# An mLSTM cell and a GELU feed-forward block on one core: the down projection as seven block products, and a new order for the first chunk

## The chip, the cores and the metric

The kernel runs on one core of one Trainium2 chip. The metric is the device time of an execution in microseconds. The core has TensorE (matmuls, with a separate row "PEld" for loading the stationary operand), VectorE (DVE), ScalarE (ACT), GpSimd (POOL) and SyncE (SP), which here only issues DMAs. Before the change, three runs took 579.77 us in the median (578.19 to 583.44).

## What is computed

The reference, cut to what matters:

```python
# q, k, v, o_gate: (4, 8, 768, 40); i_gate, f_gate: (4, 8, 768); B=4, H=8, S=768, D=40
for t in range(S):
    m_new = np.maximum(f_gate[:, :, t] + m, i_gate[:, :, t])
    f_stab = np.exp(f_gate[:, :, t] + m - m_new)
    i_stab = np.exp(i_gate[:, :, t] - m_new)
    C = f_stab * C + i_stab * outer(v_t, k_t)
    n = f_stab * n + i_stab * k_t
    y[:, :, t] = sigmoid(o_gate_t) * (C @ q_t) / np.maximum(np.abs(n . q_t), 1.0)
x = y.transpose(0, 2, 1, 3).reshape(3072, 320)
h = x @ w_in                                   # w_in: (320, 2048), float64
g = 0.5 * h * (1.0 + erf(h / np.sqrt(2.0)))
out = (g @ w_out).astype(np.float32)           # w_out: (2048, 320), float64
```

## The kernel before

**Chunks.** The sequence of 768 steps is cut into six chunks of 128. Within a chunk the recurrence is done as matrix products: scores between all pairs of steps, weighted by exponentials of the gates and masked to the past, plus the contribution of a state that is carried from chunk to chunk. So each chunk c has three parts: the cell (batch by batch, b = 0 to 3), the up projection of its 4 x 128 = 512 tokens with the GELU, and the down projection. The cell of chunk c+1 is computed while chunk c is projected down (for chunk 0, already while it is projected up).

**The order is written by hand.** A string of letters sets the program order of every engine (`play`, L463); there is no automatic scheduling, and every engine works through its own instructions in that order. FIRST holds the cell of chunk 0, UP_0 and DOWN_0 the projections of chunk 0 with the cell of chunk 1, DOWN (used for chunks 1 to 4) the down projection of a chunk with the cell of the next; the up projections of chunks 1 to 5 are eight U in a row, and the last chunk's down projection stands alone. For the cell of batch b: M masks on GpSimd (L289), W computes the weights as eight Exps on ScalarE (L310; in chunk 0 from a matmul that spreads rows of M, L307), T transposes keys and queries on TensorE (L323) with copies by ScalarE (L326), G is the output gate's sigmoid on ScalarE (L316), S the scores (L336) and their weighting on VectorE (L339), C the carry: state times queries (L359), new state (L354), and the state's decay on GpSimd (L372) and addition on VectorE (L373); V the values (L381, L384), Y the finishing chain (L391 on GpSimd, L393 to L398 on VectorE) and X the transposes of y into `xT` (L409, copied by VectorE L410 and ScalarE L411), after which the next inputs are loaded (L122, SyncE's queue). D turns the gates' factors (L192, L202). P, K and L are the fetching of weight pieces (L230), their conversion from float64 bits to float32 (L241 to L255, VectorE and ScalarE) and the input loads; R stores M to DRAM and B loads rows of it, spread over the partitions (L133).

**Up (U, L417 to L428).** One step computes two column blocks of 128 hidden units for 512 tokens: five blocks of 64 rows, alternating between the two halves of the array, into two PSUM banks of 512 columns; ScalarE writes the Gelu of both into `g`, whose layout is (128 hidden units, 16 blocks f, 512 tokens).

**Down (F, L432 to L461).** In chunk 0 a step is one block f for four batches, since the weights arrive block by block (L440). From chunk 1 on a step is four blocks of one batch (L455): 16 matmuls of 128x128 by 128x320 add up in one bank, ScalarE copies it out (L447) and SyncE stores it. That is 16 steps, 64 matmuls a chunk.

**PSUM.** There are eight banks: two for transposes (`ps_tr`), two for carries and values (`ps_h`), and four (`ps_mm`, tag "mm") which scores, up steps and down steps take in turn.

Of the kernel before, what the change touches and what calls it, by code (L numbers as in the profile page):

```python
# [21 lines left out]

FIRST = """
    W0 T0 P W1 W2 D L1 P K M0 P P T1 S0 V0 M1 L2 R C0 K S1 G0 V1 M2 K G1 T2 Y0 K G2 X0 W3 L3 K S2 L4 C1 B4 V2 Y1 X1
    T3 G3 M3 Y2 B5 S3 L5 C2 B7 V3 K C3 Y3 B6 X2 X3"""
UP_0 = """
    M0 T0 K G0 U L6 W0 S0 M1 C0 W1 M2 T1 M3 U K K U S1 V0 W2 L8 C1 U K W3 T2 K U K L7 Y0 K U U K K U T3 G1 V1 L9 S2
    G2 S3 K C2 V2 K Y1 F F Y2 X0 F K F F K K X1 F K C3"""
DOWN_0 = """
    V3 K F K F X2 F F F F G3 K K K F F Y3 K F X3 F"""  # L30
DOWN = """
    M0 T0 W0 F F M1 M2 T1 W1 W2 F S0 C0 F M3 T2 W3 G0 G1 G2 G3 F S1 C1 V0 Y0 F F T3 F S2 C2 V1 Y1 F
    X0 F S3 C3 V2 Y2 F X1 F V3 Y3 F X2 F F X3 F"""
# [3 lines left out]
def kernel(  # L37
# [31 lines left out]
    NLD = 6  # L69
    NM = 4  # L70
    NB = 4
    WP = 512
    assert S % L == 0 and DFF % (4 * WP) == 0 and DM % R == 0 and DM <= WP and D <= DP and NLD > B == NM == 4
# [9 lines left out]
    ps_mm = ctx.enter_context(tc.tile_pool(name="ps_mm", bufs=4, space=bass.MemoryType.PSUM))  # L83
# [27 lines left out]
    M_d = dram.tile([NCH - 1, BH, L], F32, name="M_d")  # L111
# [15 lines left out]
    def load_M(n):  # L127

        if n >= NCH * B:
            return  # L130
        c, b = divmod(n, B)
        Mb[n] = wts.tile([P, H, L], F32, name="Mb", tag="Mb", bufs=NM)
        nc.sync.dma_start(out=Mb[n].rearrange("p h l -> p (h l)"),  # L133
                      in_=M_d[c - 1, b * H:(b + 1) * H, :].rearrange("h l -> (h l)").unsqueeze(0).to_broadcast([P, H * L]))
# [34 lines left out]
    for c0, c1 in ((0, 1), (1, NCH)):  # L169
# [5 lines left out]
        for c in range(c0, c1):  # L175
            nc.vector.tensor_tensor_scan(out=M[:, c], data0=a[:, c], data1=a[:, c], initial=m0[:, c:c + 1],
                                         op0=OP.max, op1=OP.max)
            if c + 1 < NCH:
                nc.vector.tensor_tensor(out=m0[:, c + 1:c + 2], in0=bl[:, c, L - 1:L], in1=M[:, c, L - 1:L],
                                        op=OP.add)  # L180
    nc.vector.tensor_tensor(out=ew, in0=a[:, 0:NCH - 1],
# [32 lines left out]
    for f0 in range(0, DFF, 2 * WP):  # L214
        for blk in range(NK):
            src = w_src["in"][blk * R:(blk + 1) * R, 2 * f0:2 * (f0 + 2 * WP)]
            pieces.append(([src[:, 2 * WP * e:2 * WP * (e + 1)] for e in range(2)], w_in[:, blk, f0 // 2:f0 // 2 + WP]))
# [52 lines left out]
    def store_M():  # L270
        nc.sync.dma_start(out=M_d.rearrange("c p l -> p c l"), in_=M[:, 1:NCH])
# [7 lines left out]
    class Cell:  # L279
# [6 lines left out]
        def mask(self, b):  # L286

            t, fill = (Mb[self.c * B + b], 1.0e30) if self.c > 0 else (W[b], 0.0)
# [3 lines left out]
        def weights(self, b):  # L292
# [3 lines left out]
            if self.c > 0:  # L296
                M_n = Mb.pop(n)
            for h in range(H):
                r = b * H + h
                if self.c > 0:  # L300
# [215 lines left out]
```

## Time and profile before

| what | value |
|---|---|
| median of three runs | 579.77 us |
| the profiled execution | 579.88 us |
| its span, first to last instruction | 578.2 us |
| granted clock of TensorE (mean) | 0.999 |
| up projections start (chunks 0 to 5) | 61.92, 152.43, 241.17, 329.90, 418.64, 505.51 us |
| last chunk's down projection starts | 540.04 us |

A row of the timeline gives start, duration, engine, line, operation, what is written from what, shapes and count, and in brackets what ended the idle time before it. A float32 matmul appears as two rows of MATMUL (and two of LDWEIGHTS), since it is done in two passes; a transpose appears as one. Durations of matmuls include the time in the array and overlap, so distances between starts say more than durations. The windows view gives the busy time of each engine in a stretch.

### The profile page before, as it was taken

What the parts mean: (1) busy time and instruction counts of PE and PEld (TensorE: products, weight loads), DVE (VectorE), ACT (ScalarE), POOL (GpSimd) and SP (SyncE); (2) the same over time, 40 slices, a digit from 0 to 9 for tenths busy, and PEclk for the clock granted to TensorE, in tenths of its full rate; (3) what the DMA queues carried; (4) which work ended last, traced back from release to release, by engine and by line L of the source; (5) the groups of instructions that cost most, each with busy time, mean ns of one, the idle gap of its engine ahead of it and who ended that gap; (6) DMA issues with size and microseconds to landing.
All of it is one profiled execution on the core that took longest, in us unless ns stands there. A gap on an engine that the chain in (4) does not pass through costs nothing.

```text
span 578.2 us, 9535 instructions
## 1 busy us (share of the span) xinstructions
PE 558.8 (97%) x3914; PEld 365.5 (63%) x3914; DVE 200.8 (35%) x444; ACT 238.8 (41%) x524; POOL 82.1 (14%) x130
## 2 busy tenths in 40 slices
PE   5888899999999999999999999999999999999997
PEld 4877654776544777644778644677744677744675
DVE  6387586699300146300137300136400035300000
ACT  3567899544422841232850223750232761232100
POOL 3212320123000122300112300032300001000000
PEclk9999999999999999999999999999999999999999
DMA  9839979669300325700225800126100000000000
GB/s 158 144 84 189 238 175 207 136 133 194 70 1 0 118 62 83 115 1 1 86 73 93 126 0 1 56 103 92 24 11 1 0 14 12 12 12 1 0 23 24
DMA packets 110396, 41.54 MB, mean 72 GB/s; under 512 B 101168, under 2 KB 104400, under 8 KB 110352
## 3 DMA queue, kind: packets, MB, share of 16 engines
q1 hardware_dynamic: 110352, 40.92, 35.7%
q8 instruction: 31, 0.51, 0.4%
q14 instruction: 13, 0.11, 0.1%
HBM read 36.90 MB, written 4.01 MB: 71 GB/s over the span
## 4 chain that ended last, share of the span: by engine, by line
PE 90%; DVE 6%; ACT 2%; issue 1%; DMA 0%; SPq 0%; DVEq 0%; ACTq 0%
PE pu L425 35%; PE po L455 31%; PE ps L336 5%; PE ph L381 4%; PE pt L323 4%; PE po L440 3%; PE pm L307 2%; PE px L409 2%; PE pf L359 2%; PE pf L354 2%; DVE sig L248 1%; DVE pow L253 1%; DVE W L339 1%; DVE w_out L255 1%; DVE sig L246 0%
## 5 line engine op out<-in xcount | busy, mean ns | idle before, releaser
L425 PE MATMUL pu<-xT,w_in 64*128 64x512 f32 x960 | 209.9, 591 | 0.5 <-ACT g L428 0.4
L455 PE MATMUL po<-w_out,g 128*128 128x320 f32 x640 | 183.2, 436 | 0.0
L425 PEld LDWEIGHTS pu<-xT,w_in 64*128 64x128 f32 x960 | 94.5, 187 | 111.2 <-issue 106.9
L455 PEld LDWEIGHTS po<-w_out,g 128*128 128x128 f32 x640 | 117.4, 190 | 44.2 <-issue 0.8
L339 DVE TENSOR_TENSOR W<-ps,W 128x512 f32<-128x512 f32 x48 | 30.8, 685 | 245.4 <-PE ps L336 239.7
L428 ACT ACTIVATE g<-pu 128x512 f32<-128x512 f32 x96 | 52.1, 594 | 126.9 <-PE pu L425 126.8
L411 ACT COPY xT<-px 64x384 f32<-64x384 f32 (+1 forms) x48 | 17.9, 420 | 101.4 <-DVE xT L410 101.4
L372 POOL TENSOR_TENSOR state<-state,dec 64x164 f32<-64x164 f32 x32 | 15.1, 470 | 254.1 <-PE pf L359 252.9
L310 ACT ACTIVATE W<-Mb,aT 128x128 f32<-128x128 f32 x160 | 48.4, 392 | 0.1
L391 POOL TENSOR_TENSOR ob<-hs,ob 128x320 f32<-128x320 f32 x24 | 19.9, 829 | 135.9 <-ACT ob L316 70.5
L440 PE MATMUL po<-w_out,g 128*128 128x320 f32 x128 | 35.9, 435 | 0.8 <-DVE w_out L255 0.8
L381 PE MATMUL ph<-vb,W 128*64 128x41 f32 x768 | 29.7, 239 | 2.6 <-DVE W L339 1.5
L336 PEld LDWEIGHTS ps<-qT,kT 64*128 64x128 f32 x384 | 26.3, 204 | 9.3 <-issue 6.6
L447 ACT COPY o_sb<-po 128x320 f32<-128x320 f32 x24 | 10.1, 425 | 53.1 <-PE po L455 38.2
L336 PE MATMUL ps<-qT,kT 64*128 64x128 f32 x384 | 30.8, 302 | 0.7 <-ACT qT L326 0.7
L381 PEld LDWEIGHTS ph<-vb,W 128*64 128x64 f32 x768 | 27.2, 148 | 5.9 <-DVE W L339 2.7
L440 PEld LDWEIGHTS po<-w_out,g 128*128 128x128 f32 x128 | 23.8, 190 | 10.5 <-DVE w_out L255 1.3
L410 DVE COPY xT<-px 64x384 f32<-64x384 f32 (+1 forms) x48 | 20.9, 475 | 14.7 <-PE px L409 14.3
L243 ACT ACTIVATE pow<-pow,e_hi 128x320 f32<-128x320 uint32 (+1 forms) x26 | 16.2, 623 | 17.4 <-DVE pow L241 17.4
L289 POOL TENSOR_SCALAR_AFFINE_SELECT Mb<-Mb 128x1024 f32<-128x1024 f32 x20 | 22.7, 1160 | 2.9 <-DMA Mb<-M_d 2.7
L409 PE MATMUL px<-ident,ob 128*128 128x128 f32 x120 | 18.6, 287 | 4.1 <-DVE ob L397 3.8
L326 ACT COPY kT<-pt 128x512 f32<-128x512 f32 x24 | 14.0, 582 | 17.5 <-PE pt L323 17.4
(78 smaller groups left out, 433.1 us busy)
## 6 DMA issues: line engine op xcount, KB each, us to landing
Mb<-M_d SPq DMA_DIRECT2D x20, 512.0 KB, 3.9
bits<-in_moe_w_in_dram SPq DMA_DIRECT2D x20, 256.0 KB, 5.1
bits<-in_moe_w_out_dram SPq DMA_DIRECT2D x16, 320.0 KB, 3.4
qb<-in_q_dram SPq DMA_DIRECT2D x24, 160.0 KB, 4.3
kb<-in_k_dram SPq DMA_DIRECT2D x24, 160.0 KB, 4.7
vb<-in_v_dram SPq DMA_DIRECT2D x24, 160.0 KB, 5.2
ob<-in_o_gate_dram SPq DMA_DIRECT2D x24, 160.0 KB, 3.7
out_dram<-o_sb SPq DMA_DIRECT2D x24, 160.0 KB, 1.8
```

The lines of the kernel that those rows point to most:

```text
L289: nc.gpsimd.affine_select(out=t, in_=t, compare_op=OP.is_ge, fill=fill, base=0, pattern=[[0, H], [1, L]], channel_multiplier=-1)
L310: nc.scalar.activation(out=W[n][:, h, :], in_=src, func=AF.Exp, scale=-1.0, bias=aT[:, self.c, r:r + 1])
L323: nc.tensor.transpose(pt[:, p, :], src[n % NLD][:, 2 * p:2 * p + 2, :].rearrange("p h d -> p (h d)"), ident)
L336: nc.tensor.matmul(ps[hip][:, p, :], kT[r, p, :], qT[r, p, :], start=True, stop=True)
L339: nc.vector.tensor_tensor(out=w, in0=ps[hip], in1=w, op=OP.mult)
L381: nc.tensor.matmul(ph[r, h, :], Pm[:, h, r], vb[n % NLD][:, h, :], start=True, stop=True)
L409: nc.tensor.transpose(px[:, k, :], ob[n % NLD][:, (k0 + k) * R:(k0 + k + 2) * R], ident)
L410: nc.vector.tensor_copy(out=xT[0:R, k0:k0 + m, t], in_=px[0:R])
L425: nc.tensor.matmul(pu[e], w_in[r, blk, i * P:(i + 1) * P], xT[r, (blk - e) % NK, :], start=(blk == 0), stop=(blk == NK - 1))
L428: nc.scalar.activation(out=g[:, f + e * (WP // P), :], in_=pu[e], func=AF.Gelu)
L440: nc.tensor.matmul(hold["po"][b], g[:, f, b * L:(b + 1) * L], w_out[:, f, :], start=(f == 0), stop=(f == NF - 1))
L455: nc.tensor.matmul(po, g[:, f, b * L:(b + 1) * L], w_out[:, f, :], start=(f == 0), stop=(f == NF - 1))
```

## The change

The down projection of chunks 1 to 5 is done as a product of matrices in two-by-two blocks with seven block products in place of eight. The block rows are the two halves of the 512 tokens (h), the inner blocks the two halves of the 16 hidden blocks (e, eight each), the block columns the two halves of the 320 outputs (n). One block product is, for each of two token groups t, eight matmuls of 128x128 by 128x160, so 7 x 2 x 8 = 112 matmuls; a step F is one product for one t, and there are 14.

- After each up step VectorE forms three sums of 128x256: s1 = a21 + a22, then a11 - a21 in place of a21, then s2 = s1 - a11. They live in the four buffers that held raw weight bits. A fourth, a12 - s2 (two instructions of 128x1024), is formed in place after the second product that is read out by ScalarE (`p2`).
- After chunk 0, `weight_sums` forms the four combinations of w_out's blocks: 32 sums of 128x160 on VectorE.
- The products use two banks under tag "b", two products after one another adding into one bank: P1 then P2, P6 alone, P5 then P3, P7 then P4. What is read out in between: `p1` and `p2` are copies on ScalarE, `p6`, `p5`, `p7`, `p3` and `p4` are additions on VectorE. Outputs are stored for two batches at once, after P3 and after P4.
- PSUM: the four banks of tag "mm" become two of tag "a" (scores, even up steps, half of chunk 0's output) and two of tag "b" (odd up steps, products, the spread rows of M, the transposes X of chunk 0).
- Block f of `g` and the pieces of w_in are renumbered, so that an up step gives blocks i and i + 8.
- Input buffers are five instead of six (NLD), buffers for the spread rows of M two instead of four (NM). M_d gets a sixth block, stored on ScalarE's queue before its first Exp. (The loads that would follow it are empty, since BY_PE names all four batches.)
- FIRST, UP_0, DOWN_0 and DOWN are new strings. The number of each kind of step is as before, but for F in DOWN (14 for 16) and the early loads L and B (eight and two for nine and four, with the smaller numbers of buffers).

The diff, cut (new lines of the strings as an example):

```diff
 FIRST = """
-    W0 T0 P W1 W2 D L1 P K M0 P P T1 S0 V0 M1 L2 R C0 K S1 G0 V1 M2 K G1 T2 Y0 K G2 X0 W3 L3 K S2 L4 C1 B4 V2 Y1 X1
+    W0 D P L1 T0 T1 P M0 P K W1 S0 C0 W2 V0 G0 K R G1 L2 P M1 S1 L3 M2 L4 T2 G2 Y0 W3 V1 B4 K S2 V2 K C1 G3 M3 X0 Y1
...
 DOWN = """
-    M0 T0 W0 F F M1 M2 T1 W1 W2 F S0 C0 F M3 T2 W3 G0 G1 G2 G3 F S1 C1 V0 Y0 F F T3 F S2 C2 V1 Y1 F
-    X0 F S3 C3 V2 Y2 F X1 F V3 Y3 F X2 F F X3 F"""
+    M0 T0 W0 F F M1 T1 W1 F F S0 C0 M2 T2 W2 M3 W3 G0 G1 G2 G3 F F S1 C1 V0 Y0 F F T3 S2 C2 V1 Y1 F F X0 S3 C3 V2 Y2
+    F X1 V3 Y3 F X2 F X3 F"""
...
-    NLD = 6
-    NM = 4
+    NLD = 5
+    NM = 2
...
-    ps_mm = ctx.enter_context(tc.tile_pool(name="ps_mm", bufs=4, space=bass.MemoryType.PSUM))
+    ps_mm = ctx.enter_context(tc.tile_pool(name="ps_mm", bufs=2, space=bass.MemoryType.PSUM))
...
+        if c0 == 0:
+            nc.scalar.dma_start(out=M_d[0], in_=M[:, 0])
...
-            ps = [ps_mm.tile([P, NP, L], F32, name="ps", tag="mm") for hip in range(2)]
+            ps = [ps_mm.tile([P, NP, L], F32, name="ps", tag="a") for hip in range(2)]
...
+    def weight_sums():
+        parts = [raw.tile([P, 3, HD], F32, name="t4", tag=tag) for tag in ("sig", "pow", "sig")]
+        T[4] = lambda j: parts[j // 3][:, j % 3, :]
+        for n, x, y in ((1, Bm[0][1], Bm[0][0]), (3, Bm[1][1], Bm[0][1]), (2, Bm[1][1], T[1]), (4, Bm[1][0], T[2])):
+            for j in range(HF):
+                nc.vector.tensor_tensor(out=T[n](j), in0=x(j), in1=y(j), op=OP.subtract)
...
+            pu = [ps_mm.tile([P, TG], F32, name="pu", tag="ab"[i % 2]) for e in range(2)]
...
+            if c > 0:
+                (a11, a21), (_, a22) = [[g.t[:, i + HF * e, HT * h:HT * (h + 1)] for h in range(2)] for e in range(2)]
+                s1, s2 = [t[i // (HF // 2)][:, i % (HF // 2), :] for t in (g.s1, g.s2)]
+                nc.vector.tensor_tensor(out=s1, in0=a21, in1=a22, op=OP.add)
+                nc.vector.tensor_tensor(out=a21, in0=a11, in1=a21, op=OP.subtract)
+                nc.vector.tensor_tensor(out=s2, in0=s1, in1=a11, op=OP.subtract)
...
+        def product(lhs, rhs, k, first, t, then):
+            if first and t == 0:
+                bank[k] = ps_mm.tile([P, 2, HD], F32, name="po", tag="b")
+            for j in range(HF):
+                nc.tensor.matmul(bank[k][:, t, :], lhs(j, t), rhs(j), start=(first and t == 0 and j == 0),
+                                 stop=(t == 1 and j == HF - 1), skip_group_check=True)
+            if t == 1:
+                then(bank[k])
...
+        def p1(pb):
+            nc.scalar.copy(out=keep("p1"), in_=pb)
+        def p6(pb):
+            add(keep("u"), "p1", pb)
+        def p2(pb):
+            nc.scalar.copy(out=block(0, 0), in_=pb)
+            for i in range(2):
+                a12 = g.t[:, HF + HF // 2 * i:HF + HF // 2 * (i + 1), 0:HT]
+                nc.vector.tensor_tensor(out=a12, in0=a12, in1=g.s2[i], op=OP.subtract)
+        def p5(pb):
+            add(keep("p1"), "u", pb)
...
+        todo = ((A(0, 0), Bm[0][0], 0, True, p1), (Sm(g.s2), T[2], 1, True, p6),
+                (A(1, 0), Bm[1][0], 0, False, p2), (Sm(g.s1), T[1], 2, True, p5),
+                (A(0, 1), T[3], 3, True, p7), (A(1, 0), Bm[1][1], 2, False, p3),
+                (A(1, 1), T[4], 3, False, p4))
+        return [lambda x=x, t=t: product(*x[0:4], t, x[4]) for x in todo for t in range(2)]
```

Below, "product 1" to "product 7" are P1 to P7 of this table, in the order 1, 6, 2, 5, 7, 3, 4.

How it moves the instructions, at three places. The rows are those of the built programs: line, operation, written from read, shape and count; the names are the tiles of the code with a number where there are several. First TensorE at the start of a down projection (chunk 1), before:

```order
L455 MATMUL po<-w_out,g 128x320 x8
L323 MATMUL pt<-ident,kb_110 128x128 x4
L323 MATMUL pt<-ident,qb_104 128x128 x4
L455 MATMUL po<-w_out,g 128x320 x4
L336 MATMUL ps<-qT,kT 128x128 x8
L354 MATMUL pf<-vw,kb_109 64x41 x8
L359 MATMUL pf<-state_97,qT 64x82 x8
L455 MATMUL po<-w_out,g 128x320 x4
L323 MATMUL pt<-ident,kb_111 128x128 x4
L323 MATMUL pt<-ident,qb_105 128x128 x4
L455 MATMUL po<-w_out,g 128x320 x4
L336 MATMUL ps<-qT,kT 128x128 x8
```

and after the change (L504 once for a product's two steps F), where L504 are the products, L329 the transposes, L342 the scores, L360 and L365 the carry:

```order
L504 MATMUL po<-w_out,g 128x160 x16
L329 MATMUL pt<-ident,kb_110 128x128 x4
L329 MATMUL pt<-ident,qb_105 128x128 x4
L504 MATMUL po<-w_sums_199,sums 128x160 x16
L342 MATMUL ps<-qT,kT 128x128 x8
L360 MATMUL pf<-vw,kb_109 64x41 x8
L365 MATMUL pf<-state_97,qT 64x82 x8
L329 MATMUL pt<-ident,kb_106 128x128 x4
L329 MATMUL pt<-ident,qb_101 128x128 x4
L504 MATMUL po<-w_out,g 128x160 x16
L342 MATMUL ps<-qT,kT 128x128 x8
L360 MATMUL pf<-vw,kb_110 64x41 x8
```

One F between two cell steps has become a pair, and the third transposes follow the first carry at once.

ScalarE in the same stretch, before (L326 are the copies of T, L310 the Exps of W, L316 the gates, L447 the copy of an output):

```order
L326 COPY kT<-pt 128x512
L326 COPY qT<-pt 128x512
L310 ACTIVATE W<-Mb,aT 128x128 x16
L447 COPY o_sb<-po 128x320
L326 COPY kT<-pt 128x512
L326 COPY qT<-pt 128x512
L310 ACTIVATE W<-Mb,aT 128x128 x8
L316 ACT_TABLE_LOAD
L316 ACTIVATE ob_121<-ob_121 128x320
L316 ACTIVATE ob_122<-ob_122 128x320
L316 ACTIVATE ob_123<-ob_123 128x320
L316 ACTIVATE ob_124<-ob_124 128x320
```

and after, where L526 is the copy of product 1 and L532 that of product 2:

```order
L332 COPY kT<-pt 128x512
L332 COPY qT<-pt 128x512
L316 ACTIVATE W<-Mb,aT 128x128 x8
L332 COPY kT<-pt 128x512
L332 COPY qT<-pt 128x512
L316 ACTIVATE W<-Mb,aT 128x128 x16
L322 ACT_TABLE_LOAD
L322 ACTIVATE ob_119<-ob_119 128x320
L322 ACTIVATE ob_120<-ob_120 128x320
L322 ACTIVATE ob_116<-ob_116 128x320
L322 ACTIVATE ob_117<-ob_117 128x320
L532 COPY o_sb<-po 128x2x160
```

The copy of product 2 now stands behind all Exps and gates of the next cell. What the products that come after it wait for, as the program has it: first products 2 (the first row) and 5 (the last),

```order
L504 MATMUL po<-w_out,g 128x160 x16
L342 MATMUL ps<-qT,kT 128x128 [waits DVE_49] x2
L342 MATMUL ps<-qT,kT 128x128 x6
L360 MATMUL pf<-vw,kb_110 64x41 [waits Pool_49]
L360 MATMUL pf<-vw,kb_110 64x41 x7
L365 MATMUL pf<-state_98,qT 64x82 x8
L387 MATMUL ph<-vb_114,W 64x41 [waits DVE_49,PE_49]
L387 MATMUL ph<-vb_114,W 64x41 x15
L504 MATMUL po<-w_sums_198,sums 128x160 x16
```

then product 7 with what precedes it:

```order
L360 MATMUL pf<-vw,kb_106 64x41 x7
L365 MATMUL pf<-state_99,qT 64x82 x8
L387 MATMUL ph<-vb_115,W 64x41 [waits DVE_49]
L387 MATMUL ph<-vb_115,W 64x41 x15
L504 MATMUL po<-w_out,g 128x160 [waits Activation_49]
```

Product 5 has no wait of its own and takes the bank that product 6 left; product 7 waits for ScalarE, and takes the one that product 2 left.

Third, TensorE at the end of FIRST and in the first part of UP_0, before:

```order
L381 MATMUL ph<-vb_116,W 64x41 x16
L354 MATMUL pf<-vw,kb_110 64x41 x8
L409 MATMUL px<-ident,ob_121 128x128 x5
L409 MATMUL px<-ident,ob_122 128x128 x5
L323 MATMUL pt<-ident,kb_111 128x128 x4
L323 MATMUL pt<-ident,qb_105 128x128 x4
L425 MATMUL pu<-xT,w_in 128x512 x10
L336 MATMUL ps<-qT,kT 128x128 x8
L354 MATMUL pf<-vw,kb_111 64x41 x8
L359 MATMUL pf<-state_97,qT 64x82 x8
L323 MATMUL pt<-ident,kb_112 128x128 x4
L323 MATMUL pt<-ident,qb_106 128x128 x4
```

and after (L460 are the up steps):

```order
L415 MATMUL px<-ident,ob_119 128x128 x5
L329 MATMUL pt<-ident,kb_110 128x128 x4
L329 MATMUL pt<-ident,qb_105 128x128 x4
L460 MATMUL pu<-xT,w_in 128x512 x10
L329 MATMUL pt<-ident,kb_106 128x128 x4
L329 MATMUL pt<-ident,qb_101 128x128 x4
L342 MATMUL ps<-qT,kT 128x128 x8
L460 MATMUL pu<-xT,w_in 128x512 x10
L360 MATMUL pf<-vw,kb_110 64x41 x8
L365 MATMUL pf<-state_97,qT 64x82 x8
L387 MATMUL ph<-vb_115,W 64x41 x16
L460 MATMUL pu<-xT,w_in 128x512 x10
```

The first up step is now followed by transposes and scores, which take the banks that this up step has filled.

123 lines of the change are left out of this document (76 added, 47 removed).

## The prediction

> **What bounds the kernel now.** I read the page's busy shares and its chain of waits first, then the windows stage by stage, then TensorE's timeline.
>
> ```profile
> PE 558.8 (97%) x3914; PEld 365.5 (63%) x3914; DVE 200.8 (35%) x444; ACT 238.8 (41%) x524; POOL 82.1 (14%) x130
> ...
> PE 90%; DVE 6%; ACT 2%; issue 1%; DMA 0%; SPq 0%; DVEq 0%; ACTq 0%
> ```
>
> TensorE is busy for 97% of the span and holds 90% of the chain that ended last. The windows say where anything else counts (columns: stretch, length, then busy time and instructions of PE, PEld, DVE, ACT and POOL):
>
> ```profile
> 20.00:62.00 42.00, 33.97 (x339) 29.74 (x337) 32.27 (x67) 26.51 (x56) 10.80 (x12) 1.00 0.82 135
> 50.00:62.00 12.00, 8.22 (x110) 6.88 (x108) 10.63 (x23) 7.43 (x16) 5.02 (x6) 1.00 1.18 206
> 62.00:152.43 90.43, 89.20 (x652) 58.59 (x652) 69.28 (x155) 61.06 (x120) 18.02 (x23) 1.00 0.82 166
> 152.43:186.97 34.54, 34.54 (x162) 15.41 (x161) 0.00 (x0) 9.73 (x17) 0.00 (x0) 1.00 0.06 20
> 152.43:241.17 88.74, 88.74 (x662) 56.69 (x661) 23.62 (x52) 32.80 (x76) 14.18 (x20) 1.00 0.33 67
> 418.64:505.51 86.87, 86.87 (x597) 54.82 (x597) 19.27 (x44) 32.36 (x75) 3.22 (x4) 1.00 0.02 8
> ```
>
> Up to 62 us the first cell is computed, and TensorE idles for 8.0 of 42 us. From 62 to 152.43 (chunk 0's projections with the second cell) it idles for 1.2. Then come chunks 1 to 4, the first and the last of which are shown: no idle time at all in 88.74 and 86.87 us, while VectorE works for 23.62 and ScalarE for 32.80 of the 88.74. In the up projection, the first 34.54 us of a chunk, VectorE does nothing. So from chunk 1 on TensorE's time taken out is time gained, unless a wait appears. One chunk's instructions there (columns: start, length, count):
>
> ```profile
> 186.97 0.66 PE L323 MATMUL pt<-ident,kb 128*128 128x128 f32 x4
> 187.46 0.60 PE L323 MATMUL pt<-ident,qb 128*128 128x128 f32 x4
> 187.90 4.47 PE L455 MATMUL po<-w_out,g 128*128 128x320 f32 x16
> ...
> 202.99 1.16 PE L336 MATMUL ps<-qT,kT 64*128 64x128 f32 x16
> 204.08 0.67 PE L354 MATMUL pf<-vw,kb 128*64 128x41 f32 x16
> 204.57 0.77 PE L359 MATMUL pf<-state,qT 128*64 128x82 f32 x16
> 205.17 1.08 PE L381 MATMUL ph<-vb,W 128*64 128x41 f32 x32
> 206.18 4.57 PE L455 MATMUL po<-w_out,g 128*128 128x320 f32 x16
> 210.59 0.60 PE L323 MATMUL pt<-ident,kb 128*128 128x128 f32 x4
> 211.03 0.60 PE L323 MATMUL pt<-ident,qb 128*128 128x128 f32 x4
> ...
> 540.04 34.72 PE L455 MATMUL po<-w_out,g 128*128 128x320 f32 x128
> ```
>
> A float32 matmul shows as two passes (a chunk's 64 matmuls of the down projection are 128 rows), a transpose as one. The last chunk's 128 passes of 320 columns take 34.72 us, 271 ns each, or 270 once the tail of the last one is left out: 34.6 us a chunk. In chunks 1 to 4 they are cut into 13 runs with cell work between them. A run pays a little for the change of kind: from 206.18 to 210.59 are 4.41 us, 0.09 more than 16 x 0.270.
>
> **The change, term by term.** *The products.* In each chunk from 1 on, 64 matmuls of 320 columns become 7 x 2 x 8 = 112 of 160, so 128 passes become 224, each with its own weight load. The trace has no full pass of 160 columns at full rate. From below, half of 270 is 135 ns. Nearest in shape is the transpose, a pass of 128 columns over the whole array: four take 211.03 - 210.59 = 0.44 us, 110 ns each. The line through 110 at 128 columns and 270 at 320 gives 137 at 160. What could spoil it are the weight loads (busy, mean ns):
>
> ```profile
> L455 PEld LDWEIGHTS po<-w_out,g 128*128 128x128 f32 x40 | 7.3, 190 | 2.6
> L336 PEld LDWEIGHTS ps<-qT,kT 64*128 64x128 f32 x64 | 3.8, 187 | 0.9 <-issue 0.9
> ...
> L323 PEld LDWEIGHTS pt<-ident,kb 128*128 128x128 f32 x12 | 1.4, 141 | 1.2 <-issue 0.8
> ```
>
> A load lasts 190 ns in the down projection, 187 in the scores and 141 in the transposes: all longer than the new pass. Yet transposes follow every 110 ns, and here are 32 score passes, alternating between the halves of the rows:
>
> ```profile
> 108.11 2.06 PE L336 MATMUL ps<-qT,kT 64*128 64x128 f32 x32
> 110.10 0.67 PE L354 MATMUL pf<-vw,kb 128*64 128x41 f32 x16
> ```
>
> They take 1.99 us, 124 ns for a pair that brings two loads of 187. So loads overlap one another and the stream, and 190 is a latency, not a period. That pair is 17 ns above its columns (128 x 270/320 = 107-108), change of kind included: my upper bound is 135 + 15 = 150. I take 137, from the row nearest in shape. A chunk's down projection goes from 34.6 us to 224 x 0.137 = 30.7, 3.9 less; the new schedule has 9 runs for 13, four changes of at most 0.09 fewer, which I take as 0.2: **4.1 us less** (at 135 and 150 ns 4.6 and 1.2).
>
> [...]
>
> *The added sums.* VectorE gets three sums of 128x256 after each up step (24 a chunk), 32 of 128x160 once after chunk 0, and in each down projection two of 128x1024 and five additions of a bank of 320.
>
> ```profile
> 206.82 0.50 DVE L384 TENSOR_TENSOR hs<-ph,far 128x328 f32<-128x328 f32 x1
> ```
>
> By this row of 328 columns out of PSUM, 256 columns are 0.39 us at most by size, 160 are 0.25 and 1024 are 1.6 (0.5 each for the first two if nothing scales). The 24 sums then take 9.4 us (12) and the 32 others 8 (16), under 34.5 us of up projection in which VectorE idles; the second product, which reads the last of them, starts 5 us after it. The seven others are 5.7 us on an engine that is three quarters free. Cost: nothing; uncovered, the 24 would cost 9 us a chunk.
>
> *The banks.* The seven products rotate through two banks, and three of the four banks' contents are read out while another product is to land there or take the bank. I put the instructions in the order that the program has them, with these rows beside those above, and count from the chunk's first transpose (186.97 before):
>
> ```profile
> 187.07 1.08 ACT L428 ACTIVATE g<-pu 128x512 f32<-128x512 f32 x2 [3.21 <-PE pu L425]
> ...
> 193.80 4.79 ACT L310 ACTIVATE W<-Mb,aT 128x128 f32<-128x128 f32 x16
> ...
> 203.98 1.28 ACT L316 ACT_TABLE_LOAD   x1
> 205.28 1.55 ACT L316 ACTIVATE ob<-ob 128x320 f32<-128x320 f32 x4
> ```
>
> Product 1 needs the bank of the last Gelu's first half: free at 0.7 us, wanted at 0.9, behind eight transposes. Product 2 adds onto product 1's bank at 13.8; ScalarE copies that out behind the first eight Exps, at 6.4. Product 5 takes, at 21.4, the bank that VectorE read at 11.5 (its instructions have no wait of their own). Product 7, at 30.0, waits for ScalarE's copy of product 2, and that copy is late: with two mask buffers in place of four the third mask stands behind the state's products on GpSimd,
>
> ```profile
> 197.77 1.00 POOL L372 TENSOR_TENSOR state<-state,dec 64x164 f32<-64x164 f32 x2 [53.47 <-PE pf L359]
> 198.84 1.09 POOL L289 TENSOR_SCALAR_AFFINE_SELECT Mb<-Mb 128x1024 f32<-128x1024 f32 x1
> ```
>
> which need the first carry, done at 13.1. So the mask is ready at 15.3, and after 16 Exps (4.79), a table load (1.28), four gates (1.55) and the copy (some 0.5) it is 23.5: 6.5 us before product 7. Stores and loads queued on SyncE behind product 3's and 4's results serve the next chunk. At the end the last batch's transposes stand one F closer to VectorE's finishing chain, which now has one more addition in it: for buffers not yet copied I count 0.5 us (bounds 0 and 1.5). Chunks 1 to 4 gain 4.1 - 0.5 = 3.6 us each, **14.4** together.
>
> *The last chunk.* Nothing stands between its up and down projection, so product 1 waits for the Gelu: 0.75 us. It ends with an addition and two stores where a copy and one store stood:
>
> ```profile
> 575.30 0.33 SPq L448 DMA_DIRECT2D out_dram<-o_sb  x1
> ```
>
> One issue more and a slightly longer addition make 0.4 us. 34.6 - 30.7 - 0.75 - 0.4 = **2.8 us** gained.
>
> *The first chunk.* Every step before chunk 1 is reordered; its matmuls stay (chunk 0's down projection keeps 64 of 320 columns). Idle time is the ceiling of what an order can bring: 8.0 us from 20 to 62 and 1.2 after it, of which 0.83 stands before this row:
>
> ```profile
> 145.23 4.57 PE L440 MATMUL po<-w_out,g 128*128 128x320 f32 x16 [0.83 <-DVE w_out L255]
> ```
>
> For a gain: the decays and second transposes come before the later weights and fill early gaps. Against it: VectorE, which the finishing chains and weight conversions pass one by one, is busy for 10.63 of the last 12 us before the up projection; and scores, even up steps and half of chunk 0's output share two banks where four served all. At four places (the first two scores, the third up step, the first row of F) TensorE comes to a bank that waits for a pair of Gelus (1.08) or a table load and the Gelus (2.4); with the transposes between, some 0.5 to 1.2 us each. The store of the first block of M on ScalarE's queue finds M ready before ScalarE's first Exp. I take 1 us lost; bounds are half of the idle time, 4 gained, and 5 lost.
>
> **Sum.** The profiled execution took 579.88 us, 578.2 of span and 1.7 around it; the median of the runs is 579.77, so nothing is corrected. 579.9 - 14.4 - 2.8 + 1 = **563.7 us**, 2.8% less.
>
> **Rivals.** *Weight loads stop hiding (slower).* The place is every pass of the products. If a load can begin only when the pass before it begins, and must end before its own, the period is 190 ns once the columns take less: 1120 x (190 - 137) = 59 us more, 623 us. It turns the sign from 137 + 16.2 us/1120 = 151 ns on. For it: the 190 ns row, and that no such load ever had less than 270 to hide under. Against it: transposes every 110 with loads of 141, score pairs every 124 with two of 187. Chance 0.07. [...]
>
> *Passes somewhat dearer.* At 145 ns, halfway to the upper bound, 1120 x 8 = 9 us of the gain go: 573. For it: the scores' 17 ns above their columns; against it: the transposes' 2. Chance 0.1.
>
> *The first chunk or a bank costs more.* The first chunk loses 5 us (568), or the late copy meets its product after all, by 2.1 us if it were product 5 that takes that bank, in four chunks (572). For it: VectorE's 10.63 of 12; against it: 6.5 us of slack. Chance 0.15.
>
> *The first chunk gains.* Half of the idle 8 us goes: 559. Against it: two banks for four. Chance 0.1.
>
> That the products are not done as said is excluded by the order of the built program, with its 112 matmuls of 160 columns a chunk.
>
> **How the numbers follow.** The forecast has 0.58, with 560 to 567 as its own range. The gain reaches down to 556 with passes of 135, the losses and dearer passes up to 573: 556 to 573 leaves out the slower rival and the ends of two others. About 1%, 5.8 us, is what a measurement of this kernel tells from no change. Faster by more (below 574) are the forecast, the gain and nearly all of the two milder losses: 0.85. Within 1%: their ends, 0.08. Slower: 0.07.
>
> **What would show it right or wrong.** In the profile after: 1120 passes of products, some 30.7 us in the last chunk; 85.1 us from one up projection to the next in chunks 1 to 3; VectorE's sums inside the up projection, and TensorE not waiting for them; no idle time before product 7; chunk 1's up projection starting at 149 to 157 us. Passes above 151 ns, or over 4 us of idle TensorE in a chunk, would make the prediction wrong.

## The result, and the profile after

| | before | changed |
|---|---|---|
| median | 578.98 us (4 runs, 577.22 to 583.44) | 555.04 us (4 runs, 551.59 to 560.28) |
| ratio | | 0.956, 95% interval 0.948 to 0.964 |
| profiled execution, its span | 579.88, 578.2 us | 560.28, 558.6 us |
| up projection of chunk 1 starts | 152.43 us | 150.65 us |
| from there to the end | 425.8 us | 408.0 us |

The change makes the kernel 4.4% faster by this ratio, which compares means and leaves out the execution of 560.28 us, more than 1.5% above the fastest of its kernel; the medians alone lie 4.1% apart. 563.7 us was forecast, so the time lies 8.7 us below the forecast and 1 us below the range. The profiled execution is the slowest of its four; the same kernel profiled in another execution started chunk 1's up projection at 145.92 us and took 408.0 us from there. Everything from chunk 1 on is the same in both to 0.1 us, so the profile after can be read from that point on; the front, which is all that TensorE does before the first up projection, is taken up behind it.

The page's busy shares and chain of waits after:

```profile
PE 536.9 (96%) x4394; PEld 398.1 (71%) x4394; DVE 281.5 (50%) x631; ACT 233.8 (42%) x514; POOL 83.7 (15%) x127
...
PE 90%; DVE 7%; issue 1%; ACT 1%; DMA 0%; DVEq 0%
```

TensorE has 22 us less work in 480 more passes, and still holds 90% of the chain; VectorE went from 200.8 to 281.5 us. The windows (stretch, length, then busy time and count of PE, PEld, DVE, ACT, POOL) say that it cost nothing:

```profile
150.65:235.72 85.07, 84.87 (x757) 63.72 (x757) 43.27 (x109) 32.81 (x76) 14.17 (x20) 1.00 0.26 59
...
488.67:523.96 35.29, 34.61 (x162) 15.41 (x161) 8.80 (x22) 8.60 (x17) 0.00 (x0) 1.00 0.03 10
...
488.67:558.60 69.93, 65.30 (x385) 45.86 (x384) 14.81 (x32) 9.88 (x19) 0.00 (x0) 1.00 0.04 15
```

From chunk 1's up projection to chunk 2's are 85.07 us instead of 88.74, and TensorE idles for 0.20 of them. VectorE works for 8.80 us, nearly all of it the sums, in an up projection in which it did nothing, and the last chunk, from its up projection to the end, takes 69.93 instead of 578.2 - 505.51 = 72.69. The timeline of the last chunk's products (start, duration, count; in brackets the wait before):

```profile
523.96 4.61 PE L504 MATMUL po<-w_out,g 128*128 128x160 f32 x32 [0.68 <-ACT g L463]
528.41 4.51 PE L504 MATMUL po<-w_sums,sums 128*128 128x160 f32 x32
...
541.45 8.86 PE L504 MATMUL po<-w_out,g 128*128 128x160 f32 x64
550.14 4.51 PE L504 MATMUL po<-t,g 128*128 128x160 f32 x32
```

192 passes lie between the first row's start and the last's: (550.14 - 523.96)/192 = 136.4 ns a pass, the change of kind included. There is one wait, 0.68 us on the last Gelu. The costliest groups (busy, mean ns of one, idle before) show the loads:

```profile
L504 PEld LDWEIGHTS po<-w_out,g 128*128 128x128 f32 x640 | 87.6, 190 | 2.1 <-ACT g L463 1.5
...
L467 DVE TENSOR_TENSOR sums<-g 128x256 f32<-128x256 f32 x40 | 17.0, 425 | 127.5 <-ACT g L463 127.5
```

A load still lasts 190 ns, now under a period of 136: loads do overlap one another, and a pass takes 136.4 ns where half of 270 is 135.

The late copy, and the product behind it, in chunk 1 (two engines' timelines):

```profile
207.97 0.41 ACT L532 COPY o_sb<-po 128x320 f32<-128x320 f32 x1
```

```profile
214.22 1.08 PE L387 MATMUL ph<-vb,W 128*64 128x41 f32 x32
215.23 4.61 PE L504 MATMUL po<-w_out,g 128*128 128x160 f32 x32
```

Product 2's bank is copied out by 208.4, 6.8 us before product 7 begins at 215.23, which has no wait (6.5 was forecast).

**The front.** Before the first up projection TensorE does the same passes from 11.4 us on in every kernel here that adds none (376, or 377 where the cut takes in one more). The same window, cut at that up projection, for the kernel before:

```profile
11.40:61.92 50.52, 42.49 (x376) 37.91 (x376) 32.67 (x69) 33.66 (x80) 12.90 (x14) 1.00 0.88 149
```

and for the changed kernel:

```profile
11.40:60.90 49.50, 39.96 (x376) 35.41 (x376) 33.19 (x67) 33.75 (x81) 14.75 (x15) 0.89 1.06 170
```

Idle time is length minus TensorE's busy time: 8.03 us before, 9.54 after. It rose, and the stretch still became shorter, because the same passes took 2.5 us less. Their speed can be read from any group of equal passes, such as the 64 that spread M for the Exps (L307 before, L313 after; timeline of the changed kernel):

```profile
17.90 3.78 PE L313 MATMUL pm<-M,ident 32*128 32x128 f32 x16
...
33.49 2.05 PE L313 MATMUL pm<-M,ident 32*128 32x128 f32 x16
```

The same 16 passes take 3.78 us at 17.9 and 2.05 at 33.5: TensorE runs at about half speed first and comes to full speed at 32.2 to 33.0 us here (the four transposes at 32.22 take 0.91 us, those at 32.96 0.60); later it falls back three times, for 3.4 us from 39.6 and from 46.5 and for 6.8 from 56.7. In the profiled execution of the kernel before the same passes still took 3.78 us at 40.34, and full speed came at about 51 us:

```profile
40.34 3.78 PE L307 MATMUL pm<-M,ident 32*128 32x128 f32 x16
```

This the prediction did not look at.

### The profile page after: what moved, and what is told of

Same layout as the page of the kernel before. It is cut to its first block, busy times and chain, and to the rows that moved or that the text cites. A ratio compares the mean times of both kernels' runs of the same rounds, so it can differ in the third digit from the quotient of the medians.

```text
span 558.6 us, 10684 instructions
## 1 busy us (share of the span) xinstructions
PE 536.9 (96%) x4394; PEld 398.1 (71%) x4394; DVE 281.5 (50%) x631; ACT 233.8 (42%) x514; POOL 83.7 (15%) x127
## 4 chain that ended last, share of the span: by engine, by line
PE 90%; DVE 7%; issue 1%; ACT 1%; DMA 0%; DVEq 0%
PE pu L460 37%; PE po L504 25%; PE po L484 6%; PE ps L342 5%; PE pt L329 4%; PE ph L387 4%; PE pf L365 2%; PE px L415 2%; PE pf L360 2%; PE pm L313 1%; DVE ob L403 1%; DVE W L345 1%; DVE den L401 1%; DVE xT L416 1%; DVE M L177 1%
## 5 line engine op out<-in xcount | busy, mean ns | idle before, releaser
L460 PE MATMUL pu<-xT,w_in 64*128 64x512 f32 x960 | 210.2, 594 | 0.0
L460 PEld LDWEIGHTS pu<-xT,w_in 64*128 64x128 f32 x960 | 95.9, 188 | 107.8 <-issue 106.1
L504 PE MATMUL po<-w_out,g 128*128 128x160 f32 x640 | 92.1, 301 | 0.7 <-ACT g L463 0.7
L504 PEld LDWEIGHTS po<-w_out,g 128*128 128x128 f32 x640 | 87.6, 190 | 2.1 <-ACT g L463 1.5
L467 DVE TENSOR_TENSOR sums<-g 128x256 f32<-128x256 f32 x40 | 17.0, 425 | 127.5 <-ACT g L463 127.5
L417 ACT COPY xT<-px 64x384 f32<-64x384 f32 (+1 forms) x48 | 17.9, 420 | 91.1 <-DVE xT L416 91.0
L316 ACT ACTIVATE W<-Mb,aT 128x128 f32<-128x128 f32 x160 | 48.5, 390 | 1.7 <-POOL Mb L295 1.6
L504 PE MATMUL po<-w_sums,sums 128*128 128x160 f32 x320 | 45.5, 300 | 0.0
L504 PEld LDWEIGHTS po<-w_sums,sums 128*128 128x128 f32 x320 | 43.8, 190 | 0.2
L484 PE MATMUL po<-w_out,g 128*128 128x320 f32 x128 | 35.5, 434 | 0.1
L342 PE MATMUL ps<-qT,kT 64*128 64x128 f32 x384 | 30.1, 297 | 0.8 <-ACT qT L332 0.8
L484 PEld LDWEIGHTS po<-w_out,g 128*128 128x128 f32 x128 | 23.8, 190 | 9.9 <-DVE W L345 0.6
L387 PE MATMUL ph<-vb,W 128*64 128x41 f32 x768 | 28.1, 234 | 1.9 <-issue 1.2
L342 PEld LDWEIGHTS ps<-qT,kT 64*128 64x128 f32 x384 | 25.5, 199 | 5.1 <-issue 3.3
```

The lines of the kernel that those rows point to most:

```text
L316: nc.scalar.activation(out=W[n][:, h, :], in_=src, func=AF.Exp, scale=-1.0, bias=aT[:, self.c, r:r + 1])
L342: nc.tensor.matmul(ps[hip][:, p, :], kT[r, p, :], qT[r, p, :], start=True, stop=True)
L387: nc.tensor.matmul(ph[r, h, :], Pm[:, h, r], vb[n % NLD][:, h, :], start=True, stop=True)
L460: nc.tensor.matmul(pu[e], w_in[r, blk, i * P:(i + 1) * P], xT[r, (blk - e) % NK, :], start=(blk == 0), stop=(blk == NK - 1))
L484: nc.tensor.matmul(po[b], g.t[:, f, b * L:(b + 1) * L], w_out[:, f, :], start=(f == 0), stop=(f == NF - 1))
L504: nc.tensor.matmul(bank[k][:, t, :], lhs(j, t), rhs(j), start=(first and t == 0 and j == 0), stop=(t == 1 and j == HF - 1), skip_group_che ...
```

## The experiments

The front's gain, which the prediction did not have, is what has to be explained. In short, the theory is that it comes from the new order through TensorE's speed in the first chunk; the rival is that the order gains by dependences and waits alone. The expectations say it in full, and with what numbers. Each kernel is timed against the kernel before on the same chip.

### The changed kernel again, the old order, the new order alone, and filled gaps

> The changed kernel once more, unaltered. Its profile showed 560.3 us while three other executions took 551.6 to 555.2. Theory A (first chunk): the part from chunk 1 on is fixed (338.0 us from the up projection of chunk 1 to that of chunk 5, 69.9 from there to the end), and what differs between executions, and what the forecast missed, lies before chunk 1, where TensorE's clock was below full from 40 to 67 us in that profile: an execution of about 555 has chunk 1's up projection at 144 to 147 us instead of 150.65. Theory B (passes): it starts at 150 to 151 in all executions, and the distances between up projections shrink from 85.0 to about 84.

Measured: 555.65 us (551.58 to 563.27), ratio 0.957 (0.954 to 0.960). Chunk 1's up projection starts at 145.92, 4.7 us earlier than in the profile after. The front's window of this execution:

```profile
11.40:56.05 44.65, 37.95 (x377) 33.32 (x377) 32.29 (x67) 33.14 (x81) 12.03 (x13) 0.73 1.08 178
```

Against the profile after, the same program has 2.0 us less busy and 2.8 less idle time in the front.

```profile
17.87 2.06 PE L313 MATMUL pm<-M,ident 32*128 32x128 f32 x16
```

These 16 passes ran at full speed, some 15 us earlier than in the profile after; half speed was back from 24.7 to 28.2 us and, but for one stretch of 3.4 us, from 31.6 to 58.9. So one kernel's executions differ before chunk 1 alone, and TensorE's speed changes at other times in them. That this makes the whole spread of 551 to 563 is not shown: more of the difference between these two is idle than busy time.

The second has the seven products with the old strings FIRST, UP_0 and DOWN_0, less the loads B6, B7 and L9 that the smaller numbers of buffers leave no room for.

> Seven products as in the change, but the order of all steps before chunk 1 as it was before (without the early loads that five and two buffers do not allow). Theory A: the new order is worth what is missing in the sum, so this is 2 to 7 us slower than the changed kernel, 557 to 562 us. Theory B: within 2 us of the changed kernel.

Measured: 571.4 us (569.51 to 573.12), ratio 0.986 (0.983 to 0.989); chunk 1 starts at 160.62, 8.2 us later than before. Timeline:

```profile
41.89 3.78 PE L313 MATMUL pm<-M,ident 32*128 32x128 f32 x16 [2.60 <-ACT xT L417]
...
64.40 1.33 PE L415 MATMUL px<-ident,ob 128*128 128x128 f32 x5 [5.27 <-ACT xT L417]
```

In the old order, two banks for the spread of M and the transposes of y (with the smaller numbers of buffers, which were not tried by themselves) are not enough: TensorE waits 2.60 and 5.27 us until ScalarE has emptied one of them. Idle time in the front goes from 8.03 to 13.66 us (11.40 to 67.36 with 42.30 busy), and 2.8 us more are lost from there to chunk 1.

The third is the kernel before with the new strings (and B6, B7 and L9 kept).

> The other half: the down projection and the four common banks as before, the new order before chunk 1. Theory A: 2 to 7 us below the kernel before, 572 to 577 us. Theory B: within 2 us of it, or slower.

Measured: 573.01 us (572.06 to 573.43), ratio 0.988 (0.985 to 0.991); chunk 1 starts at 144.62, 7.8 us earlier than before. The front's window:

```profile
11.40:55.65 44.25, 35.44 (x376) 30.96 (x376) 33.70 (x67) 33.04 (x81) 15.47 (x15) 0.76 1.08 197
```

Busy time is 7.1 us less than before for the same 376 passes, idle time 0.8 more. So the order alone brings 7 to 8 us (6.9 by the medians, 7.8 by chunk 1's start), of which 6.3 lie in the front, and there not by removing waits; the 1.5 us from the front to chunk 1 are 1.2 us of idle time and some busy time. With the split banks and fewer buffers the new order starts chunk 1 at 145.92: they cost 1.3 us in it, which is less than two executions of one kernel differ by, and 8.2 in the old one.

The fourth puts products that nobody reads (identity by identity, 128 columns) into the pauses of the new order:

```diff
-    ... S2 V2 K C1 G3 M3 X0 Y1 L5 Y2 B5 C2 X1 T3 K S3 L6 C3 V3 X2 Y3 X3
+    ... S2 Z5 V2 K C1 G3 M3 X0 Y1 L5 Y2 B5 Z4 C2 Z8 X1 T3 Z4 K S3 L6 C3 Z2 V3 X2 Y3 Z14 X3
```

> The changed kernel with 37 extra matmuls of 128x128 by 128 columns, whose results nobody reads, in front of six steps of the first cell before which TensorE idles (1.2, 0.9, 1.9, 0.8, 0.5 and 3.3 us in the profile). If the clock falls because of these gaps (theory A), it stays full from 33 us on: cold passes between 40 and 67 us lose their extra 5 to 6 us, 548 to 553 us, and the executions differ less. If the clock plays no part (theory B), the extra work costs 0 to 3 us: 555 to 558.

Measured: 555.84 us, in two groups (552.4 to 553.2 and 558.5 to 558.9). In the profiled one, of 558.52, full speed came at about 33 us and then stayed to the up projection, whose first 20 passes took 4.66 us at full speed (5.95 in the changed kernel run again). Filling keeps TensorE at full speed here, and by the medians (555.84 against 555.65) it costs in time what that saves.

### Early products, and the old order changed in parts

If TensorE's speed carries the gain, full speed that comes early should bring more. The first two kernels put 16 such products into TensorE's idle time ahead of `gates_turned([(a, aT)])`, in the changed kernel and in the one with filled gaps.

```diff
+    warm(16)
     gates_turned([(a, aT)])
```

> The changed kernel with 16 products more (identity by identity, 128 columns, kept by nobody) issued on TensorE ahead of the gates' first transposes, where TensorE otherwise waits until 6.8 us; nothing else is moved. Theory A (the first chunk's gain is TensorE's clock: when it first becomes full in an execution decides, and passes that use all rows raise it): the passes of the Exps' table run at full speed before 17.9 us (2.06 us for 16 of them instead of 3.78) in every execution, there is no group of executions near 559 to 563, the up projection of chunk 1 starts at 143 to 146 us in the profile, and the median is 551 to 554. Rival B (the order brings its gain by dependences alone and the clock goes its own way): no change, a median of 555 to 556 with the same spread of 551 to 563, start at 146 to 151.

Measured: 554.93 us (552.23 to 563.39), ratio 0.959 (0.955 to 0.963). The profiled execution, of 552.23, has the fastest passes of all, and chunk 1 at 142.59:

```profile
11.40:53.84 42.44, 32.60 (x376) 28.76 (x377) 33.53 (x67) 33.17 (x81) 13.07 (x13) 0.81 1.11 188
```

But the median is where it was, nearer to B, and an execution of 563 is still there. A expected early full speed in every execution and no such group; that failed.

> The changed kernel with the same 16 early products and also products of that kind in the gaps of the first chunk's cell (as in the run that filled the gaps alone, 555.8 us). Theory A: full speed from about 10 us to the first up projection without a break, all executions in one group, median 548 to 552; the cover of the gaps costs some 2 to 4 us of TensorE where the filling is longer than the wait, and the half-speed stretch of 31 to 58 us, which costs 5 to 8, is gone. Rival B: 555 to 556, as with the gaps filled alone. Rival C (filling keeps the clock but costs what it saves): the clock is full throughout, yet the median is 553 to 557.

Measured: 555.18 us, in two groups again (552.7 to 553.1 and 557.3 to 558.0). That is the time of B and C, and the reason of neither: C expected full speed throughout. In the profiled one, of 557.34, TensorE is busy from 3.13 us, reaches full speed by 9.7, and still falls back and works at half speed from about 15 to 32 us, though no pause from 10 us up to there is longer than 0.51 us:

```profile
9.72 2.03 PE L319 MATMUL pm<-M,ident 32*128 32x128 f32 x16
...
16.77 3.78 PE L319 MATMUL pm<-M,ident 32*128 32x128 f32 x16
...
32.60 2.05 PE L319 MATMUL pm<-M,ident 32*128 32x128 f32 x16
```

So in this execution early work did not hold the speed, and the speed fell without a long pause.

The next two are the kernel before in its old order, with one part changed.

```diff
-    W0 T0 P W1 W2 D L1 P K M0 P P T1 S0 V0 M1 ...
+    W0 D P L1 T0 T1 P K M0 P P W1 W2 S0 V0 M1 ...
```

> The kernel before, with one part of the new order alone: decays, the loads of cell 1 and both first turns (D L1 T0 T1, 16 transposes of 128 rows) are issued ahead of the second and third cell's Exps' tables (W1 W2); banks, buffers, the rest of the order and the seven-product form stay as before. Theory A: the dense full-row run lets the clock become full by 18 to 22 us instead of 50.5 in most executions; the up projection of chunk 1 starts at 145 to 149 us instead of 152.4, the median is 573 to 577. Rival B: the other steps of the order carry the gain; the median stays at 578 to 580, and so does the start at 151 to 153.

Measured: 581.37 us (577.42 to 584.05), ratio 1.004 (1.001 to 1.007); both missed, the part alone loses a little. The 32 passes at 17.86 ran at full speed (4.17 us), as A said, but half speed was back by 22 and, but for a stretch at 35 to 38 us, stayed to the up projection; the front is no better than before, with 43.21 us busy and 8.12 idle:

```profile
11.40:62.73 51.33, 43.21 (x377) 38.16 (x377) 35.74 (x72) 34.55 (x82) 14.10 (x15) 0.63 0.94 159
```

> The kernel before in its old order, with 16 early products in the idle time before 6.9 us and 20 more of the same kind after the first turn, which lie on TensorE's path and cost 4.3 us at half speed or 2.1 at full speed. Theory A: the clock is full by about 14 us, the 32 passes of the Exps' table that took 7.2 us take 4.1, and what follows to 50 us runs faster wherever TensorE holds it up: median 573 to 578 in spite of the paid products. Rival B: nothing is gained and the paid products are lost, 581 to 584.

Measured: 582.61 us (580.81 to 586.09), ratio 1.008 (1.005 to 1.010): B's number. The 32 passes took 3.83 us, as A said, but the 20 paid products, 40 passes, took 6.36 us (4.3 or 2.1 was expected, the price of 20 passes), stood at 15.01 behind a wait of 2.00, and full speed was lost again by 26. What A gains the products cost, so this run does not decide between the two.

### One exchange in the new order, one more in the old, and covered waits

Theory A in its second form (A2): the order brings TensorE's speed where it leaves no pause between 13.5 and 31 us.

```diff
-    ... W1 S0 C0 W2 V0 G0 K R ...
+    ... W1 S0 C0 V0 W2 G0 K R ...
```

> The changed kernel with one exchange in its new order: the first cell's values (V0) are issued ahead of the third half of the Exps' table (W2), which covered their wait; the work is the same. Theory A2 (the new order gains because TensorE has no pause between 13.5 and 31 us, and the clock, once full, stays so only without pauses; the idle time itself is worth little): a pause of 0.6 to 0.9 us on the weighted scores appears at about 21 us, the passes behind it fall to half speed within some us, the time before the first up projection rises by 3 to 7 us, of which the pause itself is under 1; median 558 to 562. Rival B2 (only the pauses themselves count): 555.5 to 556.5.

Measured: 560.57 us (555.73 to 563.92), ratio 0.968 (0.964 to 0.972), 1.2% or 5 us above the changed kernel's 0.957 and outside its interval, for one exchange of two steps. The front in its profiled execution, the slowest:

```profile
11.40:64.39 52.99, 44.87 (x376) 39.77 (x376) 31.94 (x67) 33.96 (x81) 13.53 (x15) 0.96 1.00 161
```

The time fits A2 and not B2. The path to it is not as A2 said: the new pause is 0.15 us, and full speed was not lost behind it but had not come before, and came only at 53 us. So this execution ran at half speed already ahead of the exchange, where the run again was at full speed with the same steps, and the difference between those two is not the exchange's alone. The profile after is the fairer pair, since it too is at half speed up to the exchange: there full speed came at 32.2, and this front is 3.5 us longer, with 4.9 more busy and 1.4 less idle. Both are the slowest of their kernels' executions.

The same cover in the old order, on top of the turns ahead:

```diff
-    W0 D P L1 T0 T1 P K M0 P P W1 W2 S0 V0 M1 L2 R C0 K S1 ...
+    W0 D P L1 T0 T1 P K M0 P P W1 S0 C0 W2 V0 M1 L2 R K S1 ...
```

> The kernel before with the first turns moved ahead, as in the run that did that alone (581.4 us), and with the half table W2 and the carry C0 now issued between the first scores and the first values, so that they cover the wait at 24 us; the rest of the order, the banks and the products as before. Theory A2: no pause from 13.5 to about 28 us, full speed through it in most executions, median 574 to 578. Rival B2: the covered pause of 0.8 to 0.9 us alone, 580 to 581. Rival D (the gain lies in other steps of the order, such as the third cell's earlier masks and tables): 579 to 582.

Measured: 577.59 us (573.71 to 583.55), ratio 0.996 (0.994 to 0.998): in A2's interval, 3.8 us under the kernel without it. Front and one timeline row:

```profile
11.40:58.63 47.23, 40.18 (x376) 35.58 (x376) 37.32 (x72) 34.15 (x82) 14.24 (x15) 0.67 1.01 174
```

```profile
21.02 2.05 PE L307 MATMUL pm<-M,ident 32*128 32x128 f32 x16
```

Full speed lasts from 17 to 27 us instead of 18 to 22. Of the 4.1 us that the front is shorter than without the cover, 3.0 are busy and 1.1 idle time. Against the kernel before, both steps together have 0.9 us of the new order's 6.9 (573.01 against 579.9); the rest lies in its other steps, and was not divided further.

The last kernel takes pauses out of the new order with real work (`S2 C1 V2` for `S2 V2 K C1`, and T3 ahead of C2 and X1).

> The changed kernel with two exchanges more in the first chunk: the second cell's carry (C1) is issued ahead of its values, and the fourth cell's turn (T3, 16 transposes) ahead of the third carry and the second cell's y. In the profile of the unchanged kernel run again the pauses at these places are 0.82 (values), 0.83 (third carry), 1.45 (y) and 0.91 us (scores of the fourth cell). Theory A2: three or four of these pauses shrink to 0.3 or less and the half-speed stretch from 31 us shortens: 549 to 553 in the median. Rival B2 (idle time alone counts, and VectorE's chain of finishes behind it takes most back): 553.5 to 555. Rival E (the chain on VectorE and ScalarE bounds from 31 us on, so nothing is gained): 555 to 557.

Measured: 555.73 us, in two groups (552.9 to 553.2 and 558.2 to 560.5), ratio 0.960 (0.956 to 0.965): rival E. The pauses came back at other places:

```profile
39.63 1.13 PE L387 MATMUL ph<-vb,W 128*64 128x41 f32 x32 [1.12 <-ACT hs L392]
...
44.23 0.67 PE L360 MATMUL pf<-vw,kb 128*64 128x41 f32 x16 [1.90 <-POOL vw L356]
...
52.43 0.32 PE L387 MATMUL ph<-vb,W 128*64 128x41 f32 x4 [1.72 <-ACT state L375]
```

E's reason was not tested beyond that. None of the kernels beats the changed one by more than the measurement tells.

## Why the prediction was right and wrong

**Right: the products.** 136.4 ns a pass against 137, with loads of 190 hidden; both rivals on the passes fall. The up projections of chunks 1 to 4 start 85.07 to 85.08 us apart (85.1 forecast), product 1 of the last chunk waits 0.68 (0.75), product 7 none. From chunk 1's up projection to chunk 5's are 338.02 us instead of 353.08, 15.1 less (14.4 forecast). Chunks 1 to 3 gained 3.67 each where 3.6 was taken: the late transposes cost 0.2 us where 0.5 was taken, and TensorE's work shrank by 3.87 where 4.1 was taken. Chunk 4, in which TensorE never waits, gained 4.08. The last chunk took 2.76 less (2.8). Together 17.8 us, where 17.2 was forecast. In all the kernels here with the seven products 407.9 to 408.0 us remain from chunk 1 on, and 425.7 to 425.8 in those without.

**Right that they cost nothing, a little short in size: VectorE's sums.** An addition of 256 columns took 425 ns, where 0.39 us was the most by size and 0.5 if nothing scaled, and was hidden all the same.

**Wrong: the first chunk.** The step that failed is "Idle time is the ceiling of what an order can bring", and with it "I take 1 us lost; bounds are half of the idle time, 4 gained, and 5 lost". The first chunk gained 6.5 us in the run again (chunk 1 from 152.43 to 145.92), beyond the bound, and for the most part not from idle time: of the 5.9 us before the first up projection 4.5 are busy time and 1.3 idle, and the new order alone took 7.1 us out of the *busy* time of the same 376 passes and added 0.8 to the idle time. Nearly all passes before 51 us ran at about half speed in the profiled execution of the kernel before, which its rows had shown: 16 passes of the Exps' table took 3.78 us there, and a group of four transposes 1.06 where it took 0.60 later. The prediction read the durations of such passes from later stages alone, and the share of busy time in the first 62 us as work that cannot shrink. Had it compared one group of equal passes early and late, its bound would have reached further: the fastest front here does these passes in 32.60 us of busy time where the kernel before needs 42.49.

The sign of being right that the prediction named, a start of chunk 1 at 149 to 157 us, held in the profile after (150.65) and not in the run again (145.92), whose time is near the median.

The price of the banks was real, and hidden by the order: with two and two banks and fewer buffers the old order loses 8.2 us, the new one 1.3. The rival "the first chunk gains" had the sign, at 559, with "two banks for four" against it; the order was what made two enough.

With the two terms, 579.9 - 17.8 - 6.5 = 555.6, the median of the run again.

**What stays open.** That the order acts through TensorE's speed rests on busy and idle time in the front of three pairs: new order against old, the exchange of V0 and W2 against the profile after, and the cover in the old order. Each side is one profiled execution, in the first and third pair within 0.3% of its kernel's median. The kernel before need not go the same way each time: its mean granted clock is 0.977 to 1.000 in the other executions. What decides when the speed rises is seen in part, in the last section; what ends it is not shown. Early products did not settle it, filling keeps it without profit, and the same program changes speed at 17.9 us in one execution and at 32.2 in another.

## What to carry to other kernels

Cost block products at what half the columns take, even where a weight load lasts longer than the pass, if a nearby row shows loads overlapping; here that held to 1.4 ns (136.4 against 135, under loads of 190). Before calling busy time of an engine work, compare the same pass early and late in the trace: where it takes nearly twice as long in one stage (here 3.78 us against 2.05 for 16 passes), an order can gain more there than the idle time (here 7.1 us of busy time, with 0.8 more idle), and one execution need not be typical of that stage (here chunk 1 started at 145.92 us in one and at 150.65 in another). A change that shares banks should be tried with the order that goes with it, since either alone may tell nothing of the two together: here the banks, with the fewer buffers, cost 8.2 us in the old order and 1.3 in the new one.

## What the hardware showed

The granted clock in the rows is no sure guide at the start: for 18 to 33 us of the changed kernel's profile the windows show 1.00, while 16 passes took 3.78 us there (from 24.63) and 2.05 a little later (from 33.49).

```profile
18.00:33.00 15.00, 15.00 (x117) 13.95 (x118) 4.56 (x9) 9.73 (x25) 2.56 (x3) 1.00 0.91 137
```

TensorE was busy for all of these 15 us and reached full speed only at the end of them. From its first change on, the granted clock (third number from the end) does follow the passes, and it changes at regular points. In the run again:

```profile
17.92:24.74 6.82, 6.82 (x99) 6.36 (x100) 3.59 (x6) 6.45 (x21) 1.09 (x1) 1.00 1.25 187
24.74:28.16 3.42, 3.42 (x24) 3.07 (x24) 3.33 (x6) 3.36 (x6) 2.16 (x3) 0.50 0.50 132
28.16:31.57 3.41, 3.41 (x54) 3.11 (x54) 3.20 (x8) 3.39 (x7) 0.45 (x1) 1.00 1.40 151
31.57:38.40 6.83, 5.90 (x69) 5.03 (x67) 5.90 (x9) 5.28 (x14) 3.20 (x4) 0.50 1.10 160
38.40:41.81 3.41, 1.14 (x21) 1.00 (x21) 3.03 (x12) 3.32 (x8) 1.49 (x2) 1.00 0.99 211
41.81:58.88 17.07, 14.26 (x101) 11.16 (x101) 12.23 (x25) 9.50 (x21) 4.50 (x4) 0.50 1.06 169
```

Every stretch is 3.41 us long or a multiple of that (6.82, 17.07), and in the ten other profiles here whose clock falls in the first 80 us the changes lie so too. Where these points lie differs between executions of one kernel: the first fall is at 24.74 us here and at 39.62 in the profile after, 14.88 us or 4.4 such steps later.

What lies in the 3.41 us ahead of such a point seems to matter. Between 18 and 33 us the passes use 32 or 64 of the array's rows or write 41 columns, for the most part. Ahead of them ten profiles have the decays and both first transposes, passes over all rows, in one run from about 13.5 to 17 or 18 us. In five of these a step of 3.41 us lies in that run, to within 0.12 us, as from 14.50 to 17.92 in the run again, and the passes behind it run at full speed, 16 of the Exps' table in 2.04 to 2.06 us or 32 in 4.17 (the run again, the new order alone, the early products, the old order with the turns first and with the cover). In the other five (the profile after, both kernels with filled gaps, the exchange, the covered waits) a point, counted back from later ones in steps of 3.41 us, lies at 15.1 to 16.1 us and cuts the run in two; the same 16 passes take 3.78 us behind it, and half speed stays until 32 us or later. The two kernels with early products are the same program up to 36 us and fall on different sides. In the old order with the turns first, full speed ended at 21.2 us behind 3.41 us of passes of 32 rows without a pause. This is read from the traces; no kernel here was made to test it, and why full speed ends elsewhere is not sorted by it.
